# Polysketch attention and a noisy top-2 router on one core: batch 1's query features turned through DRAM, keys-values in one step, loads in another order, two buffers for the final reads

## The chip, the cores and the metric

One core of a Trainium2 chip runs the whole program. The metric is the device time of one execution in microseconds. All arrays begin and end in DRAM.

## The reference

Attention comes first. For each of 4 batches and 4 heads there are 1088 tokens with 32 numbers in q, k and v. Two 8 x 32 sketches S1 and S2 give 8 + 8 numbers for a token, and their outer product is its 64 features:

```python
def phi(x):
    a = np.einsum('rd,bhsd->bhsr', S1, x)
    b = np.einsum('rd,bhsd->bhsr', S2, x)
    return np.einsum('bhsi,bhsj->bhsij', a, b).reshape(*x.shape[:-1], r * r)
q_p, k_p = (phi(q), phi(k))
kv = np.einsum('bhsf,bhsd->bhfd', k_p, v)
z = np.sum(k_p, axis=2)
num = np.einsum('bhsf,bhfd->bhsd', q_p, kv)
den = np.einsum('bhsf,bhf->bhs', q_p, z)[..., None] + 1e-06
return (num / den).astype(np.float32)
```

The result is laid out as x with 4352 tokens of 128 numbers. The router then adds noise to x @ w_gate, scaled by log1p(exp(x @ w_noise)), takes the best two of 8 experts for each token and softmaxes their two numbers; each chosen expert adds its weight times relu(x @ w1[e]) @ w2[e], with w1 of 128 x 1024 and w2 of 1024 x 128.

## The kernel before

The program builds a list of jobs (`Plan.add`), and then issues them in one fixed order that is written out by hand: `PLACES` is that order as job numbers, `ENGINES` the engine of each job (P for PE, D DVE, A ACT, G POOL, S for SP, which issues DMAs), `ZEROS` the number of filler matmuls that PE runs ahead of a job (`idle`, L465 to L471), and `HOLDS` the loads that wait for a given scatter. Each engine runs its own jobs in that order, one after the other. SP's queue is in order too: a DMA that waits for data keeps back all that is behind it on SP.

A batch is 8 columns of 128 tokens (t = 0 to 7) and a half column (t = 8). For each batch:

- `load_kq` and `load_v` (L373 to L392) load k and q in one DMA each and v in six; all DMAs go through one helper (L351, issued at L356).
- `turned` (L617 to L625) puts tokens along the partitions with DVE's transpose.
- `sketches` (L627 to L682) multiplies by the sketches on PE (L640, L643), copies one half out (L349), makes the other (`ab`, L657), and forms the products (L675) on DVE or POOL: `phk` and `phq`, the features of k and q.
- `keys_values` (L708 to L790) runs these, copies v into `vaug`, and multiplies features by values on PE (L757), in five steps for batch 0 and three for the others; `fold` (L775) puts the gate weights into the result `kvw`.
- The numerators (L819) want the q features turned. By default PE turns them, two transposes for a column (L807), and an engine evicts them to `pT`. For the batches in `TURNED`, `squares` (L690 to L706) does it instead: four DMAs of 128 KB write four columns to DRAM, four read them back in rows of 128 bytes, and DVE transposes 32 x 32 blocks (L703).
- `queries` (L792 to L864) divides, and forms logits.
- `router` (L920 to L1102) takes the tokens of half a batch (a group w): counts of tokens for each expert by matmul (L1009, L1012), positions (L1030), the row of each token in the experts' buffer `xs` (L1049 to L1053), weighted copies `xg` (L1065, L1067), and indirect scatters on POOL into `xs` (L1093), each behind a `step` memset (L913).

The experts work on blocks of 128 rows of one expert (`block`, L1143 to L1259). The first four blocks (u = 0 to 3, issued in the order 0, 2, 1, 3) do not wait for scatters: one-hot squares (L1155, L1156, L1159) gather their rows from x on PE (L1165). Blocks below `QUICK` = 8 load their rows `xb` in one DMA with rows of 512 bytes, transpose on PE (L1184) and evict; later blocks load in four DMAs with rows of 128 bytes and transpose on DVE (L1194). Then PE multiplies by w1 (L1204, two steps of 8 matmuls), ACT or DVE applies relu (L1212, L1210), and PE multiplies by w2 (L1219, two steps). The results go by indirect scatter into `pairs` (L1247), and `sums` (L1263 to L1286) reads both rows of a token back as `pr`, adds them (L1277), adds what late blocks left in a PSUM bank (L1237, L1281), and writes the output. `blocks` is one tile that serves the one-hot squares, `squares` and `spread` in turn; `pr` has one buffer.

Of the kernel before, what the change touches and what calls it, by code (L numbers as in the profile page):

```python
# [101 lines left out]
TURNED = (2, 3)  # L102
HOLDS = {'clear6': (1, 2, 1), 'v3': (1, 2, 1)}
PLACES = [4, 3, 20, 33, 42, 43, 44, 21, 45, 1, 48, 50, 0, 56, 60, 24, 57, 49, 53, 51, 35, 52, 18, 63, 2, 61, 62, 36,
# [1417 lines left out]
```

## Time and profile before

| what | us |
|---|---|
| median of 3 runs (338.49 to 339.95) | 339.68 |
| the profiled execution | 339.91 |
| its span | 338.2 |
| PE busy in the span | 326.5 |
| POOL busy | 239.6 |
| DVE busy | 174.4 |
| ACT busy | 121.8 |

In the rows below a PE row is a group of matmuls that run one behind the other: start, duration, line, result<-operands, number, and in brackets the idle time ahead of it and what ended that. SPq rows are DMA issues. PEclk is the granted clock of PE as a share of full speed. The DMA share is the mean busy share of the core's 16 DMA engines.

### The profile page before, as it was taken

To read this page: it belongs to the slowest core of one execution; us is meant where nothing else is said; L and a number is where in the kernel's file an instruction comes from. 1 tells how busy PE (TensorE), PEld (TensorE's weight loads), DVE (VectorE), ACT (ScalarE), POOL (GpSimd) and SP (SyncE) were. 2 spreads that over 40 slices of the span, in tenths; PEclk is the share of its full clock that TensorE was granted. 3 is DMA by queue.
4 is the path that set the end of the run, shared out by engine and by line. 5 is a ranking of instruction groups with operands and counts; after the bars stand their busy time and mean duration, and the time that the engine had idled before them with its cause. 6 is when DMAs were issued, how large, how long until landed. Compare 5 with 4: busy or idle time off the path is not lost.

```text
span 338.2 us, 8094 instructions
## 1 busy us (share of the span) xinstructions
PE 326.5 (97%) x2848; PEld 311.4 (92%) x2848; DVE 174.4 (52%) x652; ACT 121.8 (36%) x325; POOL 239.6 (71%) x396
## 2 busy tenths in 40 slices
PE   8997999999999999999999999999999999999991
PEld 5885899999999999999999999999999999999991
DVE  5679975776748675473565544420223232423342
ACT  2366677345544443531333231123322212122310
POOL 7555487894876988498858888388878647766610
PEclk9799999999999999999999999999999999999998
DMA  7999994944563664465325166214534021323451
GB/s 169 270 281 297 240 293 127 297 121 92 108 163 67 129 143 91 67 162 96 71 55 84 43 141 142 78 35 114 87 65 96 33 90 52 106 80 112 136 178 52
DMA packets 91563, 42.81 MB, mean 127 GB/s; under 512 B 67141, under 2 KB 84934, under 8 KB 91520
## 3 DMA queue, kind: packets, MB, share of 16 engines
q1 hardware_dynamic: 86880, 33.25, 43.5%
q0 software_dynamic: 4544, 8.89, 7.4%
q8 instruction: 23, 0.38, 0.5%
q14 instruction: 20, 0.16, 0.2%
q10 hardware_dynamic: 96, 0.13, 0.1%
HBM read 26.27 MB, written 16.17 MB: 126 GB/s over the span
## 4 chain that ended last, share of the span: by engine, by line
PE 73%; DMA 8%; POOL 7%; issue 5%; DVE 4%; SPq 1%; ACT 1%; POOLq 0%; DVEq 0%
PE hp L1204 30%; PE acc L1219 29%; POOL pairs L1247 5%; PE bank L819 4%; PE bank L643 4%; POOL step L913 2%; DMA out_dram<-o 2%; DMA kq<-in_q_dram 2%; PE bank L757 2%; SPq L356 1%; DMA pr<-pairs 1%; PE turn L1165 1%; DMA xb<-xs 1%; PE bank L807 1%; DVE o L1277 1%
## 5 line engine op out<-in xcount | busy, mean ns | idle before, releaser
L1219 PE MATMUL acc<-w2s,h 128*128 128x128 f32 x1152 | 145.9, 275 | 0.0
L1204 PE MATMUL hp<-bT,w1s 128*128 128x128 f32 (+1 forms) x896 | 145.5, 306 | 0.1
L1219 PEld LDWEIGHTS acc<-w2s,h 128*128 128x128 f32 x1152 | 140.5, 192 | 2.6
L1204 PEld LDWEIGHTS hp<-bT,w1s 128*128 128x128 f32 x896 | 121.2, 192 | 5.0 <-ACT bT L349 0.4
L1212 ACT ACTIVATE h<-hp 128x512 f32<-128x512 f32 x104 | 62.0, 598 | 122.2 <-PE hp L1204 107.4
L1093 POOL DMA_INDIRECT xs<-xg,to x72 | 71.6, 994 | 34.8 <-issue 10.5
L1247 POOL DMA_INDIRECT pairs<-y,mine x70 | 69.7, 996 | 34.7 <-ACT y L349 18.2
L913 POOL MEMSET step<- 1x512 f32 x142 | 73.0, 514 | 0.1
L1210 DVE TENSOR_SCALAR h<-hp 128x512 f32<-128x512 f32 x40 | 27.7, 691 | 74.0 <-PE hp L1204 52.8
L349 ACT COPY y<-acc 128x128 f32<-128x128 f32 x52 | 13.2, 265 | 41.7 <-PE acc L1219 36.4
L1194 DVE STREAM_TRANSPOSE bT<-xb 128x128 f32<-128x128 f32 (+1 forms) x48 | 16.3, 347 | 7.0 <-PE hp L1204 3.8
L819 PE MATMUL bank<-kvw,pT 128*128 128x98 f32 x128 | 16.7, 272 | 0.0
L1065 ACT ACTIVATE xg<-x,g 128x128 f32<-128x128 f32 x49 | 16.0, 394 | 0.0
L819 PEld LDWEIGHTS bank<-kvw,pT 128*128 128x128 f32 x128 | 15.7, 192 | 0.0
L349 DVE COPY y<-acc 128x128 f32<-128x128 f32 x18 | 5.0, 282 | 18.7 <-PE acc L1219 18.1
L657 DVE TENSOR_TENSOR ab<-bank,lo 128x256 f32<-128x256 f32 (+2 forms) x17 | 6.3, 380 | 8.9 <-ACT lo L349 8.8
L1277 DVE TENSOR_TENSOR o<-pr 128x512 f32<-128x512 f32 (+1 forms) x12 | 6.5, 544 | 7.7 <-DMA out_dram<-o 6.1
L643 PE MATMUL bank<-sk,qTs 128*128 128x128 f32 x64 | 10.0, 296 | 0.0
L675 DVE TENSOR_TENSOR phq<-ab 128x512 f32<-128x512 f32 (+1 forms) x13 | 9.3, 717 | 0.1
L643 PEld LDWEIGHTS bank<-sk,qTs 128*128 128x128 f32 x64 | 8.9, 210 | 0.0
L471 PE MATMUL turn<-const-bfloat16-1.0 128*128 128x512 bf16 (+2 forms) x26 | 7.7, 447 | 0.9 <-PEq L1505 0.9
L349 ACT COPY pT<-bank 128x512 f32<-128x512 f32 (+1 forms) x12 | 6.2, 516 | 4.5 <-PE bank L807 4.4
(184 smaller groups left out, 277.5 us busy)
## 6 DMA issues: line engine op xcount, KB each, us to landing
w1s<-in_moe_w_dram SPq DMA_DIRECT2D x8, 512.0 KB
w2s<-in_moe_w_dram SPq DMA_DIRECT2D x8, 512.0 KB
pr<-pairs SPq DMA_DIRECT2D x8, 512.0 KB
kq<-in_k_dram SPq DMA_DIRECT2D x4, 544.0 KB
kq<-in_q_dram SPq DMA_DIRECT2D x4, 544.0 KB
vld<-in_v_dram SPq DMA_DIRECT2D x16, 128.0 KB
xb<-xs SPq DMA_DIRECT2D x128, 16.0 KB
there<-phq SPq DMA_DIRECT2D x16, 128.0 KB
```

The lines of the kernel that those rows point to most:

```text
L349: A.copy(o, i) if e == "ACT" else V.tensor_copy(o, i)
L643: T.matmul(ps.t[rows, 2 * W * i:2 * W * i + 2 * W], lhsT=lhsT, rhs=sk[:].rearrange("p c h x -> p (c h x)"), start=True, stop=True)
L819: T.matmul(ps2.t[:, c0:c0 + 2 * YW], lhsT=pT.t[:, at + P * (2 * i + a):at + P * (2 * i + a) + P], rhs=kvw.t[:, a, :], start=True, stop=True)
L913: job.fill = G.memset(step[:], 0.0)
L1065: A.activation(out=xg.t[:, i, c, 0:D], in_=x.t[:, c, :], func=AF.Copy, scale=B_["g"].t[:, i, c:c + 1])
L1093: ins = G.indirect_dma_start(out=xs[:], in_=xg.t[rows, i, t, :], in_offset=None, out_offset=bass.IndirectOffsetOnAxis(ap=to.t[rows, i, t:t ...
L1194: add("DVE", vec(P * n), lambda _: V.transpose(bT.t[:, 0:P * n], flat()), r=[xb], w=[bT], prio=TOP + u)
L1204: T.matmul(hp.t[:, P * n * i:P * n * (i + 1)], lhsT=w1s[:, e, P * (js * g + i):P * (js * g + i + 1)], rhs=bT.t[:, 0:P * n], start=True, st ...
L1210: V.tensor_scalar_max(h.t[:], hp.t[:], 0.0)
L1212: A.activation(out=h.t[:], in_=hp.t[:], func=AF.Relu)
L1219: T.matmul(acc.t[:, D * c:D * c + D], lhsT=h.t[:, P * (n * i + c):P * (n * i + c + 1)], rhs=w2s[:, e, j, :], start=(j == 0 and c == 0), st ...
L1247: ins = G.indirect_dma_start(out=pairs[:], in_=y.t[:], in_offset=None, out_offset=bass.IndirectOffsetOnAxis(ap=numbers_of[w].t[:, e, c:c + ...
```

## The change

- Batch 1 joins `TURNED`: its q features go through DRAM in two squares. `squares` and `spread` get a tile of their own (`squared`); `pr` gets a tile of its own and `blocks` as a second buffer.
- POOL products of batch 1 (`held`) wait until the index of group 0 is formed, and the index's last step (a CAST) of group 0 moves from DVE to POOL.
- Keys-values of batches 1 to 3 are one step instead of three.
- `QUICK` goes from 8 to 4: blocks 4 to 7 load in four DMAs and are transposed by DVE.
- In `sums` the adds of the PSUM banks at the end keep the order of the list (`summed`).
- `HOLDS`: v of batch 3 is no longer held, w2 of expert 7 is. `ZEROS`: 22 fillers instead of 26, at other places.
- `PLACES` and `ENGINES` are written anew. On SP, in the first 50 us: k0, q0, v0, k1, noise, w1 of expert 0, w1 of 2, a clear, w1 and w2 of 6, v1, q1, a clear, w2 of 0 and 1, k2, w2 of 3, w1 of 4 and 1, q2, the four stores of batch 1's first square with w1 of 3 among them, w2 of 2, w2 of 5, a clear. Before: k0, q0, v0, noise, w1 of 0, k1, q1, v1, w1 of 2, w2 of 1, w1 of 3, a clear, w1 of 1 and 7, w2 of 0, k2, w2 of 2, a clear, w2 of 4, a clear, the last piece of v1. (Small loads and the place of each piece of v are left out.) On PE the q features of columns 4 to 7 of batch 0 stand behind the fold instead of ahead of the keys-values. On POOL the product of columns 0 and 1 of batch 1's q features stands behind the first scatter of group 0 and two products of k features.

```diff
-TURNED = (2, 3)
-HOLDS = {'clear6': (1, 2, 1), 'v3': (1, 2, 1)}
+TURNED = (1, 2, 3)
+HOLDS = {'clear6': (4, 3, 1), 'w2_7': (0, 1, 0)}
...
-ZEROS = {44: 7.6, 50: 4.5, 153: 12, 222: 1}
+ZEROS = {44: 7.6, 66: 4.5, 72: 1.0, 153: 8}
...
-    tag("pr", 1, [P, 4, 2, D])
...
+    squared = const.tile([P, 1024], F32, name="squared")
+    kept("pr", const.tile([P, 4, 2, D], F32, name="pr"), blocks[:].rearrange("p (c k d) -> p c k d", c=4, k=2))
     kept("oh", *(blocks[:, 512 * i:512 * i + 512].rearrange("p (c x) -> p c x", c=4) for i in range(2)))
-    kept("squares", blocks[:].rearrange("p (i y x) -> p i y x", i=4, x=32))
-    kept("spread", blocks[:, 0:5 * P])
+    kept("squares", squared[:].rearrange("p (i y x) -> p i y x", i=4, x=32))
+    kept("spread", squared[:, 0:5 * P])
...
-            add(products, {"DVE": vec(256 * (m - i)), "POOL": gtt(256 * (m - i))}, product, r=list(source),
+            formed = add(products, {"DVE": vec(256 * (m - i)), "POOL": gtt(256 * (m - i))}, product, r=list(source),
                 w=[(jobs[i][2], jobs[x][1]) for x in range(i, m)], prio=prio, port={"DVE": 0.0 if whole == "PSUM" else 1, "POOL": 9})
+            if held and "POOL" in products:
+                behind_index.append(formed)
...
+            kw["held"] = b == 1
...
-        for ts in ((0, 1), (2, 3), (4, 5), (6, 7), (8,)) if head else ((0, 1, 2), (3, 4, 5), (6, 7, 8)):
+        for ts in ((0, 1), (2, 3), (4, 5), (6, 7), (8,)) if head else (tuple(range(C + 1)),):
...
-            V.tensor_copy(B_["to"].t[:, :, 0:n], B_["at"].t[:, :, 0:n])
+            if w > 0:
+                V.tensor_copy(B_["to"].t[:, :, 0:n], B_["at"].t[:, :, 0:n])
...
+        if w == 0:
+            pool_job(gps(2 * n) + 0.08, prio, lambda: G.tensor_copy(to.t[:, :, 0:n], B_["at"].t[:, :, 0:n]), [to], [B_["at"]])
+            indices.append(plan.jobs[-1])
...
-    QUICK = 8
+    QUICK = 4
+    summed = []
...
-                    in1=bank.t[rows, 0:c * D].rearrange("p (c d) -> p c d", d=D), op=ALU.add), r=[bank], w=[o], prio=prio)
+                    in1=bank.t[rows, 0:c * D].rearrange("p (c d) -> p c d", d=D), op=ALU.add), r=[bank], w=[o], prio=prio,
+                    after=summed)
+                summed.append(plan.jobs[-1])
...
+    for j in behind_index:
+        j.deps.update(indices)
     plan.write(idle)
```

## Rows read from the trace of the kernel before

**Rows 1.** The page, parts 1 and 4: busy time, chain that ended last.

```profile
PE 326.5 (97%) x2848; PEld 311.4 (92%) x2848; DVE 174.4 (52%) x652; ACT 121.8 (36%) x325; POOL 239.6 (71%) x396
...
PE 73%; DMA 8%; POOL 7%; issue 5%; DVE 4%; SPq 1%; ACT 1%; POOLq 0%; DVEq 0%
```

**Rows 2.** Windows: from:to, length, busy of each engine, PEclk, DMA share, GB/s.

```profile
2.00:50.00 48.00, 44.22 (x447) 38.14 (x446) 37.49 (x144) 26.32 (x84) 29.94 (x89) 0.96 1.00 268
...
50.00:330.00 280.00, 279.77 (x2392) 271.60 (x2389) 134.88 (x503) 94.90 (x242) 208.50 (x299) 1.00 0.45 106
...
12.00:16.00 4.00, 4.00 (x40) 3.88 (x42) 2.09 (x5) 2.23 (x7) 3.09 (x15) 0.67 1.00 340
16.00:20.00 4.00, 3.85 (x79) 3.26 (x75) 3.09 (x7) 2.16 (x6) 3.39 (x9) 1.00 0.76 233
36.00:40.00 4.00, 4.00 (x38) 4.00 (x38) 3.79 (x12) 1.49 (x7) 1.90 (x3) 1.00 0.88 191
104.00:112.00 8.00, 8.00 (x74) 8.00 (x73) 5.85 (x19) 3.37 (x10) 6.28 (x7) 1.00 0.61 101
```

**Rows 3.** Timeline of the end, PE and DVE.

```profile
330.13 1.38 PE L1237 MATMUL bank<-late_y,blocks 128*128 128x128 f32 x10 [0.35 <-ACT late_y L349]
331.01 0.69 DVE L1277 TENSOR_TENSOR o<-pr 128x512 f32<-128x512 f32 x1 [1.54 <-DMA pr<-pairs]
```

**Rows 4.** Timeline of PE, 10 to 60 us.

```profile
10.71 1.50 PE L640 MATMUL bank<-sk,qTs 128*128 128x64 f32 x8 [0.81 <-DVE qTs L623]
12.01 2.02 PE L643 MATMUL bank<-sk,qTs 128*128 128x128 f32 x8
...
21.25 1.04 PE L807 MATMUL bank<-ident,phq 128*128 128x128 f32 x8
22.12 1.95 PE L643 MATMUL bank<-sk,kTs 128*128 128x128 f32 x16
...
27.34 0.18 PE L1009 MATMUL bank<-mk,earlier 128*128 128x32 bf16 x1 [0.65 <-DVE mk L992]
...
40.99 0.86 PE L757 MATMUL bank<-phk,vaug 128*33 128x64 f32 x24 [0.65 <-issue]
...
44.78 1.06 PE L1219 MATMUL acc<-w2s,h 128*128 128x128 f32 x8
...
59.24 0.27 PE L1184 MATMUL turn<-ident,xb 128*128 128x128 f32 x1
```

**Rows 5.** Timeline of DVE: one-hot squares after the counts.

```profile
28.07 2.39 DVE L1159 TENSOR_SCALAR blocks<-place,pos,gm 128x128 f32<-128x128 f32 x3
...
38.14 0.34 DVE L1159 TENSOR_SCALAR blocks<-place,pos,gm 128x128 f32<-128x128 f32 x1
```

**Rows 6.** Timeline of SP and ACT: two issues, and the copy of v.

```profile
35.00 0.68 SPq L356 DMA_DIRECT2D vld<-in_v_dram  x1
...
39.83 1.06 ACT L349 COPY vaug<-vld 128x1024 f32<-128x1024 f32 x1 [1.24 <-DMA vld<-in_v_dram]
...
55.77 0.35 SPq L356 DMA_DIRECT2D xb<-xs  x1
```

**Rows 7.** DMA issues: what, queue, number, size of one.

```profile
w1s<-in_moe_w_dram SPq DMA_DIRECT2D x8, 512.0 KB
...
kq<-in_q_dram SPq DMA_DIRECT2D x4, 544.0 KB
...
there<-phq SPq DMA_DIRECT2D x16, 128.0 KB
...
xs<-pad SPq DMA_DIRECT2D x6, 258.0 KB
```

**Rows 8.** Timeline of POOL: group 0's first and last scatters, a product.

```profile
37.92 1.21 POOL L1093 DMA_INDIRECT xs<-xg,to  x1 [6.06 <-DVE blocks L1159]
...
40.81 1.08 POOL L675 TENSOR_TENSOR phq<-ab 128x512 f32<-128x512 f32 x1
...
51.08 0.96 POOL L1093 DMA_INDIRECT xs<-xg,to  x1 [0.17 <-issue]
```

More of the change, by code (lines that the diff above doesn't have):

```diff
@@ L194 @@
-ZEROS = {44: 7.6, 50: 4.5, 153: 12, 222: 1}
+TURNED = (1, 2, 3)
+HOLDS = {'clear6': (4, 3, 1), 'w2_7': (0, 1, 0)}
+PLACES = [20, 33, 21, 3, 4, 43, 44, 45, 29, 30, 25, 1, 26, 57, 49, 36, 48, 2, 39, 0, 56, 66, 67, 53, 54, 55, 22, 27,
[73 rows of a table added]
+ENGINES = (
+    "ASSSASSSGGGGGGSSSSSSGGGGGGGGGGGGGGGGGGGGGGDDPDAADDPADPADDDDDPADPADPADPADPADPPPPPAAPAADPDDGGPADGSSSSSSSSSSSSSSS"
+    "SSSSSSSSSSSSSSSSPAPDDADPAPDDAAAAAAGDDDDDDGAPDDGGDDGGAAAADDGGGGGGGGSDDDAADPADGGDDDPADDDPADDDDPDDGDSSSSSSSSDPAAP"
+    "AADPADDDSSSSSSSSDPAPDDPAPDDPAPDDAAAADDDDDDDDAPDDDGAADADDGGGGGGGGGGPDDPDDAAAADDDDDDDGAPDDDGADAADDGGGGGGGGPDDPDD"
+    "PAPDDAAAADDDDDDDDAPDDDGAAAADDGGGGGGGGGGSSSSSSSSAADPADDDDDDPADDDPADDDDPADDDSSSSSSSSDPDAPAADPADDDSSSSSSSSDPDDPDD"
+    "PDDPDDPAPDDAAAADDDDDDDDAPDDDGAAADAADDGGGGGGGGGGGGGGGGGGSSSSSSSSAADPADDDDDDPADDDPADDDDPDDDDSSSSSSSSDPDDPDADPADD"
+    "DSSSSSSSSDPDDPDDPDDPDDPDPDDAAAADDDDDDDDAPDDDGAAAAAADDGGGGGGGGGGGGGGGGGGGSDADDAPPPPAPAPPAPDGADDAPPPPAPAPPAPAGAA"
+    "AAPPPPAPAPPAPAGAAAAPPPPAPAPPAPAGSSSSDPAPPAPAGSSSSDPAPPAPAGSSSSDPAPPAPAGSSSSDPAPPAPAGSDDDSSSSDPAPPAPAGSSSSDPDPP"
+    "APAGSSSSDPAPPAPDGSSSSDPAPPAPDGSSSSDPAPPAPAGSSSSDPDPPAPDGSSSSDPAPPAPAGSSSSDPAPPAPAGSDDDDDDSSSSDPAPPAPAGSSSSDPDP"
+    "PAPDGSSSSDPAPPAPDGSSSSDPAPPAPAGSSSSDPAPPAPAGSSSSDPAPPAPDGSSSSDPAPPAPDGSSSSDPAPPAPDGSDSSDSSDSSDDDDDDSSSSDPAPPAP"
+    "AGSSSSDPAPPAPDGSSSSDPDPPAPAGSSSSDPAPPDPAGSSSSDPAPPAPAGSSSSDPAPPAPDGSSSSDPAPPAPAGSSSSDPAPPAPAGSSDDDDDDSSSSDPAPP"
+    "APPAPPAPAGAGSSSSDPDPPDPPAPPDPDGAGSSSSDPDPPDPPAPPDPAGDGSSSSDPAPPDPPAPPAPDGDGSSSSDPDPPAPPDPPDPAGAGSSSSDPDPPAPPAP"
+    "PAPAGAGSSSSDPAPPAPPDPPAPDGDGSSSSDPDPPDPPDPPDPDGDGSDSSDSSDSSSDDDDDDSSSSDPAPPAPPAPPAPDGDGSSSSDPDPPAPPAPPAPDGAGSS"
+    "SSDPAPPDPPDPPDPAGDGSSSSDPDPPDPPAPPDPDGAGSSSSDPAPPAPPDPPAPDGAGSSSSDPDPPAPPDPPAPDGDGSSSSDPAPPAPPAPPDPAGAGSSSSDPA"
+    "PPDPPAPPDPAGDGSDSSDSSDSSDSSSDDDDDDSSSSDPDPPDPAGSSSSDPAPPAPAGSSSSDPDPPAPAGSSSSDPAPPDPAGSSSSDPAPPAPAGSSSSDPAPPAP"
+    "AGSSSSDPAPPAPDAPPSSSSDPAPPAPDAPPSDDSSDDSA")
@@ L625, in turned, with sketches @@
         add("DVE", vec(128 * (c1 - c0) if c0 < C else 64), emit, r=[src], w=[(dst, c) for c in range(c0 // 2, -(-c1 // 2))], prio=prio)
-    def sketches(jobs, prio, whole=False, after=(), first=None, products=("DVE", "POOL"), bank="bank"):
+    def sketches(jobs, prio, whole=False, after=(), first=None, products=("DVE", "POOL"), bank="bank", held=False):
         ps = new(bank)
@@ L684 @@
     kv_of, kv_job = {}, {}
+    behind_index = []
     PQ = KNOBS
@@ L758, in emit @@
                                  start=(t == 0 and a == 0), stop=(t == C), skip_group_check=True)
-            kv_job[b] = add("PE", KV * len(ts), emit, lat=0.15, w=[kvp], prio=prio + 3.5,
+            kv_job[b] = add("PE", KV * len(ts) if head else 2.4, emit, lat=0.15, w=[kvp], prio=prio + 3.5,
                 r=[(pk, t) for t in ts] + [(va, 0), (va, 1)])
@@ L776, in fold @@
                              rhs=wg4[rows_of(l), a, :], start=True, stop=True)
-        folded = add("PE", 0.38, fold, lat=0.15, r=[kvT, "wg"], w=[ps], prio=prio + 3)
+        folded = add("PE", 0.58, fold, lat=0.15, r=[kvT, "wg"], w=[ps], prio=prio + 3)
         for l in range(2):
@@ L908 @@
     scatters = {}
+    indices = []
     def scatter_job(emit, **kw):
@@ L1052, in index @@
             V.tensor_reduce(out=B_["at"].t[:, :, 0:n], in_=B_["f2"].t[:, :, 0:n, :], axis=AX.X, op=ALU.add)
-            V.tensor_copy(B_["to"].t[:, :, 0:n], B_["at"].t[:, :, 0:n])
-        indexed = dve(0.2 + 2 * vec(16 * n), index, ["first", "row"], ["f2", "at", "to"], late)
+            if w > 0:
+                V.tensor_copy(B_["to"].t[:, :, 0:n], B_["at"].t[:, :, 0:n])
+        indexed = dve((0.2 if w > 0 else 0.0) + 2 * vec(16 * n), index, ["first", "row"], ["f2", "at"] + ["to"] * (w > 0), late)
         xg, to = B_["xg"], B_["to"]
+        if w == 0:
+            pool_job(gps(2 * n) + 0.08, prio, lambda: G.tensor_copy(to.t[:, :, 0:n], B_["at"].t[:, :, 0:n]), [to], [B_["at"]])
+            indices.append(plan.jobs[-1])
         pool_job(gps(18) + 0.1, prio, lambda: G.tensor_copy(xg.t[:, :, 0:n, D:XW].bitcast(I32), pid[:, :, b, t0:t0 + n].unsqueeze(3)),
```

16 lines of the change are left out of this document (removed), and 146 rows, old and new, of the table PLACES.

## The prediction

> **What bounds the kernel now.** I read the page first: PE is busy for 97% of the span, and the chain that ended last runs through PE for 73% and through DMA for 8% [rows 1]. The table of windows tells the two stages apart [rows 2]: from 50 to 330 us PE works 279.77 of 280 us, so there only PE work that disappears shortens the end; from 2 to 50 us it is idle for 3.8 us, and in that stage the 16 DMA engines are full (share 1.00 from 2 to 50 us, 268 GB/s). Whatever comes in this head as a wait or leaves it moves the whole later row of matmuls. The tail holds little: PE's last result needs 330.13 + 1.38 = 331.51, and DVE had the last read pairs in its hands at 331.01 [rows 3]. The profiled execution took 339.91 us, 338.2 of them the span; it stands 0.23 above the median of 339.68. I sum against 339.91 and subtract the same from 339.68.
>
> **PE work removed.** Eight transposes take 22.12 − 21.25 = 0.87 us, 0.109 each [rows 4]. Batch 1 loses 16 (columns 0 to 7 of its q features, two each), blocks 4 to 7 one each: 20 x 0.109 = **2.18 us**. Their evictions go too, off PE's path. In exchange DVE gets two transposes of a square and four of a block; DVE has 10.5 us of 48 free in the head [rows 2], so they cost nothing if the data is there; without that cover each is late by its own length. Keys-values in one step are the same matmuls: 0, between 0.65 gained (the wait ahead of the first third at 40.99 [rows 4]) and 0.65 lost if all of them now wait for the last product. Fewer fillers (26 to 22) cost or gain nothing by themselves: they stand in waits. The square's own tile lets it land while the one-hot squares are in use, v of batch 3 let loose and w2 of expert 7 held back move loads that PE needs 20 us and more later: 0.
>
> **The head.** Ahead of the counts of the first group of tiles (27.34) PE ran the q features of columns 4 to 7, 2.02 us at a low clock [rows 4], before the keys-values. They now stand behind the fold, in a stretch where PE waited or ran fillers. I take 2.0 us earlier counts, between 0 (if the values' copy holds the keys-values where they are) and 2.3. After the counts DVE formed three one-hot squares in 2.39 us beside three POOL products, where one alone took 0.34 [rows 5]: 2.39 − 3 x 0.34 = 1.37. The held products leave that stretch; I take 1.3, bounds 0 and 1.4. The index's CAST on POOL instead of DVE is 0.2 either way. The price of the hold is behind it, at the square's stores, below.
>
> PE order then reaches the w2 matmuls of the second block in order (block 2), the row at 44.78 [rows 4]. By the lists of the order, the changed kernel has done 1.2 us more PE work at that place (a w1 step of block 2 for one of block 1; two thirds of the keys-values 1.42 and two transposes of column 8, 0.22, that it has already done; less four transposes 0.44). So if X is the time at which it starts them, the end moves by X − 44.78 − 1.2 − 2.18 = **X − 48.16**, plus stalls that come later. By PE alone X = 44.78 − 2.0 − 1.3 − 0.65 + 1.2 = 42.0, a gain of 6.1.
>
> **But block 2 needs the w2 of its expert, and that is now late in SP's order.** Two things can hold it.
> First the bytes. The last v piece of batch 1 was issued at 35.00 and its copy could start at 39.83, 4.8 us later, having waited for it [rows 6]. Against what stood ahead of that piece, there stand ahead of and with block 2's w2 now four weight loads (w1 or w2 of an expert) of 512 KB more and two fewer, q of batch 2 (544), four stores of the square (128 each), and one clear less (258) [rows 7]: 1.87 MB more. At 340 GB/s, the rate from 12 to 16 us, this is 5.5 us, at the 268 of the whole head 7.0 [rows 2]: 45.3 to 46.8. Of idle DMA time 0.96 + 0.48 us can be filled (shares 0.76 and 0.88 [rows 2]): 43.9 to 45.4.
> Then the queue. SP issues in order, and the four stores of batch 1's first square, which wait for a POOL product of q features, stand in front of two weight loads. That product ended at 41.89 [rows 8], behind two scatters; now it stands behind one (some 1.65 less: 0.96, its step memset and 0.17 of issue), and what feeds it is 2.0 earlier: 38.2. Five issues of 0.43 and 4.8 to land: X = 45.2. Who waits: everything behind on SP (w1 of block 3, w2 of blocks 2 and 5), and PE. I take the later of both, X = 45.2: **−2.9**.
>
> **Later stalls.** The square's loads back have 128-byte rows. The window from 104 to 112, in which a square of batch 2 goes out and back with block loads beside it, has 0.61 x 8 = 4.9 us of all DMA engines [rows 2]; that is the upper bound for a square, the lower is 1.05 MB at 340 GB/s, 3.1. Loaded behind block 2's w2 and w2 of block 5, a clear and a piece of v, they are there about 7 us after X, with the DVE transpose; the numerators that need them come 11 us after X by PE's work: 0.
> Block 6 is next: its xb can only be read once the eight scatters of group 0 have landed. Before, the last ended at 52.04, the first read (of block 4, then first) was issued at 55.77 and transposed on PE at 59.24 [rows 4, 6, 8]. PE wants it at X + 13.5 = 58.7; it will be there between 59.5 and 3.3 us earlier. Stall 0 to 0.8: +0.4. Four issues of 0.43 where there was one lie in SP's free time.
>
> **Reads of the pairs in two buffers, ordered adds.** The second read can start before the first is added. PE's last result and the last read end within 0.5 us [rows 3], so 0, bounds ±0.3.
>
> **The clock.** PE idled 0.81 us before 10.71, and the granted clock of 12 to 16 us is 0.67 on average, so between the levels 1.2 and 2.4 GHz [rows 2, 4]: 4 x 0.33 = 1.3 us lost. It may happen again with fewer fillers or go away. From 16 to 20 us, with PE busy 3.85 of 4, it is back at 1.00 [rows 2]. I take 0, bounds ±1.3. The Trainium skill, "TensorE: Matmul & The Clock Gate", section What's actually happening, calls the throttled clock the default, which activity releases. The rows agree that it came back under work; by the rule every filler removed speaks against the change, and the sum would be −1.2 in place of −2.5; that fewer fillers lower the clock here, no run shows yet.
>
> **Sum:** −2.9 + 0.4 = −2.5: 337.4 against the profiled 339.91, **337.2** against the median. A measurement here tells 0.5% (1.7 us) from no change.
>
> **Rivals.**
> *Loads in time (0.20).* The DMA is full at 268 GB/s but moved 340 for 4 us, so the bytes ahead may pass faster, and SP may reach the stores only after the product is done. Then X = 42.0, block 6 is wanted at 55.5 and ready at 56.2 at best: −6.1 + 0.7 = −5.4, about 334.3. Against it: a share of 1.00 over the whole head.
> *Nothing reaches the end (0.22).* X = 45.4 by the lower rate, block 6 no earlier than before (59.5 instead of 58.9: +0.6) and one more drop of the clock (+1.3): −2.8 + 0.6 + 1.3 = −0.9, about 338.8. This is the change that doesn't do what it says: the transposes' 2.18 us are freed and waited away. Some 0.08 of the chance is the clock's, since the one drop before followed an idle PE.
> *Slower (0.18): SP stands at the square's stores.* POOL's first scatter waits for tiles weighed on ACT, which forms one-hot squares at that time, and the product, now behind two held products and that scatter, holds the stores, the weights behind them, and so PE. Each us that the product is late is one of PE's. It decides at a product's end of 48.16 − 7.0 = 41.2; before, it ended at 41.89 [rows 8] with counts 2 us later. If it ends at 43.0, X = 50.0: +1.8, about 341.5; the gap that then opens on PE (8 us from its own 42.0) may lower the clock and add up to 1.3. For it speaks that POOL's first scatter waited 6 us before; against it that most of what it waited for moves forward with the counts.
>
> **How the numbers follow.** Forecast 0.40 (X from 44 to 46.4, 335.5 to 338.0), the rivals 0.20, 0.22 and 0.18. All of the forecast and the first rival is faster by over 0.5%: 0.60; the second is within it, 0.22; the third 0.18. The range reaches down past the first rival's middle by 0.5 and up to just short of the slower one's: 333.8 to 341.0; it leaves out some 0.1 on either side. The forecast's own range is 335.5 to 338.0.
>
> **What would show it.** Step by step: 20 fewer transposes in the PE rows of L807 and L1184; counts at about 25.3; three one-hot squares on DVE in about 1 us; block 2's second matmuls (L1219) released by DMA of w2s, not by ACT, at about 45; the POOL product ahead of the stores ending at about 38; block 6's first matmuls at about 59 after a wait of under 1 us on a DMA or DVE transpose; from there to 329 us no idle PE. The prediction is wrong if block 2's second matmuls start before 43 or after 48, if PE waits for the numerators of batch 1, or if a stall of over 1 us appears after 65 us.

## The result, and the profile after

| | before | after |
|---|---|---|
| median (lowest to highest), us | 339.75 of 6 (338.49 to 342.61) | 335.58 of 6 (334.23 to 337.13) |
| the profiled execution | 339.91 | 335.77 |
| its span | 338.2 | 334.1 |
| end of PE's last matmul in it | 331.51 | 328.83 |
| from there to the span's end | 6.69 | 5.27 |

The ratio is 0.9878, with an interval of 0.9842 to 0.9913: faster, by more than the 0.5% that counts as a difference here. (A ratio, here and below, leaves out executions over 1.5% above the fastest of the same kernel.) Sign and range held, but the gain is 4.2 us where 2.5 were forecast. The last two lines of the table say where to look: 2.68 us come from PE's row, which the sum was about, and 1.42 from the time behind it, which the sum had put at nothing.

The lines have moved: w1 is L1214 now, w2 L1229, the keys-values L762, the numerators L824, the counts L1015, the gathers L1175, the products of features L676, the sums' adds L1289 and L1293. The page of after, parts 1 and 4, against [rows 1]:

```profile
PE 323.3 (97%) x2822; PEld 308.7 (92%) x2824; DVE 175.4 (53%) x653; ACT 125.4 (38%) x334; POOL 238.4 (71%) x398
...
PE 81%; DVE 6%; SPq 4%; DMA 4%; issue 2%; ACT 1%; POOL 0%; DVEq 0%
```

PE has 3.2 us less to do. Its part of the chain that ended last grew from 73% to 81%, while POOL's fell from 7% to 0 and DMA's from 8% to 4%. Windows of after (columns as in [rows 2]):

```profile
2.00:50.00 48.00, 44.52 (x453) 39.19 (x453) 38.98 (x151) 28.28 (x89) 32.43 (x95) 0.96 1.01 275
50.00:326.00 276.00, 275.20 (x2352) 266.94 (x2351) 134.56 (x499) 96.34 (x245) 204.78 (x294) 1.00 0.49 114
20.00:30.00 10.00, 7.37 (x45) 5.83 (x45) 9.05 (x43) 7.27 (x28) 5.37 (x14) 0.84 1.11 290
```

The head is as full of DMA as before, and PE is idle in it for 3.5 us (3.8 before). New is the third row: from 20 to 30 us PE is idle for 2.6 us, and the granted clock is 0.84 on average, so part of the time it stood at 1.2 instead of 2.4 GHz. The drop of before, at 12 us, is gone: from 10 to 20 us the clock is 1.00 in after and 0.83 in before. The timeline of PE in after shows the places, to be read against [rows 4]:

```profile
24.82 0.19 PE L1015 MATMUL bank<-mk,earlier 128*128 128x32 bf16 x1 [0.66 <-DVE mk L998]
...
26.93 0.80 PE L1175 MATMUL turn<-blocks,x 128*128 128x128 f32 x2 [1.82 <-ACT blocks L1166]
27.52 1.87 PE L824 MATMUL bank<-kvw,pT 128*128 128x98 f32 x8
...
42.48 2.21 PE L762 MATMUL bank<-phk,vaug 128*33 128x64 f32 x72
44.84 1.13 PE L1229 MATMUL acc<-w2s,h 128*128 128x128 f32 x8 [0.16 <-DMA w2s<-in_moe_w_dram]
...
58.65 1.98 PE L1214 MATMUL hp<-bT,w1s 128*128 128x128 f32 x16
...
63.88 2.02 PE L1214 MATMUL hp<-bT,w1s 128*128 128x128 f32 x16 [0.58 <-PE acc L1229]
```

Counts at 24.82 (25.3 was forecast), block 2's second matmuls at X = 44.84, released by the DMA of their weights (45.2), block 6 at 58.65 with no wait (59): the steps of the head stand where the sum put them. Not foreseen are the 1.82 us ahead of the gathers, where PE waits for a one-hot square of ACT; the eight numerators behind them take 1.87 us instead of 1.03, so the clock has fallen there. The wait that was expected at block 6 stands at block 4 instead, 0.58 us at 63.88.

Why the weights came when they came is on SP; the timeline of SP in after:

```profile
36.00 0.81 SPq L355 DMA_DIRECT2D there<-phq  x2
36.86 0.42 SPq L355 DMA_DIRECT2D w1s<-in_moe_w_dram  x1
37.33 0.91 SPq L355 DMA_DIRECT2D there<-phq  x2
38.28 1.43 SPq L355 DMA_DIRECT2D w2s<-in_moe_w_dram  x2
```

SP stood at the stores until 36.00, as the forecast had it, and went on to the w2 of block 2 at 38.28. What let it go is seen on DVE and POOL (timeline of after):

```profile
27.79 0.34 DVE L1169 TENSOR_SCALAR blocks<-place,pos,gm 128x128 f32<-128x128 f32 x1
28.15 2.08 POOL L676 TENSOR_TENSOR phk<-ab 128x512 f32<-128x512 f32 x2
28.21 1.02 DVE L1090 TENSOR_TENSOR lim<-stops,reach 128x8 f32<-128x8 f32 x1
...
33.90 2.04 DVE L676 TENSOR_TENSOR phq<-ab 128x512 f32<-128x512 f32 x1
34.30 1.08 POOL L676 TENSOR_TENSOR phq<-ab 128x512 f32<-128x512 f32 x1
```

POOL's product, which the forecast had ending at 38.2, ended at 35.38; the last one ahead of the stores was DVE's, 2.04 us long and done at 35.94. The chain that ended last goes through it (the chain of after):

```profile
33.98 1.96 DVE phq L676
46.34 4.71 DMA xs<-xg,to
55.03 4.55 DMA xb<-xs
74.67 2.23 DMA xb<-xs
```

It does not go on through the stores, w2 and X. From the product it runs through DVE's next steps to the last scatter of group 0, then through SP's reads of rows for the blocks, and comes to PE only at 77.56, at a last wait of 0.22 us. So in after the end hangs on these reads: behind the 0.16 at X they take 0.58 and 0.22 us from what PE has gained.

The two one-hot squares that DVE still makes here take 0.34 us each, as forecast for three; the held POOL products have moved on to other instructions of DVE (L1090, 1.02 us for 128 x 8 numbers). PE does not wait for these, but the product ahead of the stores does: it stands behind them on DVE, which names no wait between the counts and that product.

Last the end. Timeline of before, the rows beyond [rows 3]:

```profile
331.81 0.69 DVE L1281 TENSOR_TENSOR o<-o,bank 128x512 f32<-128x512 f32 x1
332.42 0.27 DVE L1277 TENSOR_TENSOR o<-pr 64x128 f32<-64x128 f32 x1
...
332.73 0.28 DVE L1281 TENSOR_TENSOR o<-o,bank 64x128 f32<-64x128 f32 x1
```

and of after:

```profile
327.04 0.89 DVE L1289 TENSOR_TENSOR o<-pr 64x128 f32<-64x128 f32 x2 [1.14 <-DMA pr<-pairs]
...
327.45 1.38 PE L1247 MATMUL bank<-late_y,squared 128*128 128x128 f32 x10 [0.35 <-ACT late_y L348]
327.98 0.28 DVE L1293 TENSOR_TENSOR o<-o,bank 64x128 f32<-64x128 f32 x1
...
328.87 0.69 DVE L1293 TENSOR_TENSOR o<-o,bank 128x512 f32<-128x512 f32 x1 [0.61 <-PE bank L1247]
329.59 0.66 ACTq L355 DMA_DIRECT2D out_dram<-o  x1
```

Before, the adds of the small piece stood behind those of the large one, and its output was issued last, at 333.74 (the end of SP's last issues), 2.23 us after PE's end. After, the small piece is done while PE still works, and the last issue is the large one, ended at 330.25, 1.42 after PE's end. That is 0.81 of the 1.42 us. Of it, 0.26 is the bank's add of the large piece, which follows PE's end by 0.30 before (331.81; DVE was still adding the read) and by 0.04 after (328.87). The other 0.61 is the landing of the last output: 4.46 us from that issue to the span's end before, 3.85 after.

### The profile page after: what moved, and what is told of

Read it like the earlier page. It is cut to its first block, busy times and chain, and to the rows that moved or that the text cites. A ratio compares the mean times of both kernels' runs of the same rounds, so it can differ in the third digit from the quotient of the medians.

```text
span 334.1 us, 8083 instructions
## 1 busy us (share of the span) xinstructions
PE 323.3 (97%) x2822; PEld 308.7 (92%) x2824; DVE 175.4 (53%) x653; ACT 125.4 (38%) x334; POOL 238.4 (71%) x398
## 4 chain that ended last, share of the span: by engine, by line
PE 81%; DVE 6%; SPq 4%; DMA 4%; issue 2%; ACT 1%; POOL 0%; DVEq 0%
PE acc L1229 34%; PE hp L1214 34%; SPq L355 4%; PE bank L824 3%; DMA xb<-xs 2%; PE bank L644 2%; PE turn L472 2%; DMA xs<-xg,to 1%; PE bank L762 1%; PE bank L641 1%; PE hp L641 1%; PE bank L1247 1%; DVE phq L676 1%; PE acc L762 1%; DVE phk L676 1%
## 5 line engine op out<-in xcount | busy, mean ns | idle before, releaser
L1229 PE MATMUL acc<-w2s,h 128*128 128x128 f32 x1152 | 145.4, 276 | 0.2 <-DMA w2s<-in_moe_w_dram 0.2
L1214 PE MATMUL hp<-bT,w1s 128*128 128x128 f32 (+1 forms) x896 | 144.8, 306 | 0.8 <-PE acc L1229 0.6
L1229 PEld LDWEIGHTS acc<-w2s,h 128*128 128x128 f32 x1152 | 140.1, 192 | 2.8 <-issue 0.3
L1214 PEld LDWEIGHTS hp<-bT,w1s 128*128 128x128 f32 x896 | 121.1, 192 | 5.8 <-PE acc L1229 1.1
L1257 POOL DMA_INDIRECT pairs<-y,mine x70 | 68.7, 982 | 33.5 <-issue 11.0
L1220 DVE TENSOR_SCALAR h<-hp 128x512 f32<-128x512 f32 x38 | 26.3, 691 | 65.7 <-PE hp L1214 53.5
L1204 DVE STREAM_TRANSPOSE bT<-xb 128x128 f32<-128x128 f32 (+1 forms) x52 | 17.6, 343 | 15.1 <-DMA xb<-xs 11.9
L348 ACT COPY y<-acc 128x128 f32<-128x128 f32 x42 | 10.7, 263 | 37.0 <-PE acc L1229 33.4
L1075 ACT ACTIVATE xg<-x,g 128x128 f32<-128x128 f32 x65 | 21.0, 392 | 0.3 <-DMA pairs<-y,mine 0.3
L348 DVE COPY y<-acc 128x128 f32<-128x128 f32 x28 | 7.6, 282 | 20.8 <-PE acc L1229 15.4
L824 PE MATMUL bank<-kvw,pT 128*128 128x98 f32 x128 | 17.3, 282 | 0.0
L824 PEld LDWEIGHTS bank<-kvw,pT 128*128 128x128 f32 x128 | 16.4, 201 | 0.0
L676 DVE TENSOR_TENSOR phq<-ab 128x512 f32<-128x512 f32 (+1 forms) x14 | 10.0, 723 | 0.1
L644 PE MATMUL bank<-sk,qTs 128*128 128x128 f32 x64 | 9.2, 279 | 0.6 <-DVE den L839 0.6
L644 PEld LDWEIGHTS bank<-sk,qTs 128*128 128x128 f32 x64 | 8.0, 192 | 0.9 <-PE bank L824 0.8
L707 DVE STREAM_TRANSPOSE pT<-squared 128x1024 f32<-128x1024 f32 x6 | 7.4, 1241 | 1.5 <-DMA squared<-there 0.8
L676 DVE TENSOR_TENSOR phk<-ab 128x512 f32<-128x512 f32 (+1 forms) x13 | 8.0, 614 | 0.0
```

What stands on the lines that cost most here:

```text
L348: A.copy(o, i) if e == "ACT" else V.tensor_copy(o, i)
L644: T.matmul(ps.t[rows, 2 * W * i:2 * W * i + 2 * W], lhsT=lhsT, rhs=sk[:].rearrange("p c h x -> p (c h x)"), start=True, stop=True)
L676: (G if e == "POOL" else V).tensor_tensor(out=jobs[i][2].t[rows, jobs[i][1]:jobs[m - 1][1] + 1, :, :].rearrange("p c h (i j) -> p (c h) i ...
L824: T.matmul(ps2.t[:, c0:c0 + 2 * YW], lhsT=pT.t[:, at + P * (2 * i + a):at + P * (2 * i + a) + P], rhs=kvw.t[:, a, :], start=True, stop=True)
L1075: A.activation(out=xg.t[:, i, c, 0:D], in_=x.t[:, c, :], func=AF.Copy, scale=B_["g"].t[:, i, c:c + 1])
L1214: T.matmul(hp.t[:, P * n * i:P * n * (i + 1)], lhsT=w1s[:, e, P * (js * g + i):P * (js * g + i + 1)], rhs=bT.t[:, 0:P * n], start=True, st ...
```

## The experiments

They ran on three chips, one for each group below, with the kernel before on the same chip; all edits are made to the kernel after. The kernel after as it stands ran beside them on the third chip only; where the first two groups compare with it, they compare with the result above. In the pieces of the order, a number is a job.

### First chip: what sets X, and what X is worth

**w2_ahead** issues the w1 of block 3 and the w2 of block 2 (jobs 104 and 103) ahead of the square's stores:

```diff
-633, 206, 205, 208, 210, 661, 104, 209, 196, 207, 103, 162,
+633, 206, 205, 104, 103, 208, 210, 661, 209, 196, 207, 162,
```

> The changed kernel with w1 of block 3 and w2 of block 2 issued on SP ahead of the four stores of batch 1's first square, nothing else moved. In the changed kernel SP stood at these stores until 36.00, when DVE's product ended, and PE waited 0.16 us for w2 of block 2 at 44.84. Theory (SP's stand sets that landing): the wait of PE on w2s is gone, w2 lands 2 us or more earlier, block 2's w2 matmuls start at 44.7, and the end moves by only -0.2, because PE itself came at 44.68. Rival (the bytes in front set it): the start stays at 44.8 and PE still waits on the DMA. Second rival (something else is freed): over 1 us faster.

It gave 334.05, ratio 0.9858 (0.9785 to 0.993), span 333.0. Timeline of PE:

```profile
44.99 1.16 PE L1229 MATMUL acc<-w2s,h 128*128 128x128 f32 x8
```

The wait for the weights is gone, and X has not moved forward (44.99 against 44.84): PE gets there by its own work no earlier. But the clock was low for longer in this execution (0.81 from 20 to 30 us, 0.85 from 30 to 40, against 0.84 and 0.99 in after), so PE itself came later. In after weights and PE arrive within 0.2 us of each other (the wait of 0.16).

PE's end came 1.09 us earlier all the same (327.74 against 328.83), since the later waits of after, 0.58 and 0.22 us, are not in this trace. There the chain that ended last runs on PE through the whole stretch from 60 to 83 us, and no longer through the reads. That is the second rival of the expectation (something else is freed) and not its theory. One trace of each shows it; the ratios, 0.9858 and 0.9878, don't tell the two kernels apart.

**fill** puts seven filler matmuls into the wait ahead of the gathers:

```diff
-ZEROS = {44: 7.6, 66: 4.5, 72: 1.0, 153: 8}
+ZEROS = {44: 7.6, 66: 4.5, 72: 1.0, 153: 8, 628: 7}
```

> The changed kernel with 7 more filler matmuls ahead of the first gather, in the 1.82 us in which PE idled at 25.1 to 26.9 and after which its numerators ran at about half speed (1.87 us for 8 instead of 1.03). Theory (PE and the load of w2 are tied at 44.8): the clock stays up, PE comes to block 2's w2 about 1.0 us earlier and waits there about 1.2 us; the end stays (within 0.3). Rival (the clock's fall is on the path): about 1.0 us faster.

It gave 333.3, ratio 0.9821 (0.9779 to 0.9863), span 332.1. Timeline of PE:

```profile
26.52 0.49 PE L1175 MATMUL turn<-blocks,x 128*128 128x128 f32 x2 [0.28 <-ACT blocks L1166]
26.85 1.03 PE L824 MATMUL bank<-kvw,pT 128*128 128x98 f32 x8
...
43.36 1.13 PE L1229 MATMUL acc<-w2s,h 128*128 128x128 f32 x8 [0.16 <-DMA w2s<-in_moe_w_dram]
```

The granted clock from 20 to 30 us is 1.00, the numerators take 1.03, and X moved forward by 1.48, weights included. The theory that PE would only wait longer for its weights fell: the stores go at 34.53 instead of 36.00, w2 is issued 1.41 earlier, and lands 1.48 earlier. Two things make up these 1.47 us. The counts, which stand ahead of the fillers, came 0.40 earlier in this execution (24.42 against 24.82), so that part is not the fillers'. The rest is the length of DVE's product, the last one ahead of the stores (timelines of POOL and DVE):

```profile
32.85 1.06 POOL L676 TENSOR_TENSOR phq<-ab 128x512 f32<-128x512 f32 x1 [0.42 <-DVE den L839]
33.45 1.02 DVE L676 TENSOR_TENSOR phq<-ab 128x512 f32<-128x512 f32 x1
```

In after POOL's product ran inside DVE's time and DVE's took 2.04; here it began first and DVE's took 1.02. POOL was earlier because its scatter waits for ACT (0.30 us here, 1.74 in after), and ACT for PE's transposes (its copy starts at 28.38, in after at 30.32). So the stores follow PE by way of ACT, POOL and DVE, and are not a fixed date. The span fell by 2.0 us, some 1.6 without the counts' part.

The ratios of fill and after (0.9821 and 0.9878) were not measured side by side, and their intervals overlap. The granted clock of whole executions says the same as the traces: 0.996 to 0.998 in the four of fill, 0.985 to 0.994 in the six of after; and the one execution of w2_ahead with 0.996 took 332.96.

**w2_fill** has both edits.

> Both edits: the two weight loads ahead of the stores and the 7 fillers. Theory (two limits tied): only both together pay: block 2's w2 matmuls start at about 43.7 and the end comes 1.1 us earlier than that of the changed kernel, about 334.5. Rival (bytes): start 44.8, wait on w2s of about 1 us, no gain. Rival (clock alone): as much as the fillers alone.

It gave 333.32, ratio 0.9828 (0.9785 to 0.9872), span 331.3, X at 43.13 with no wait: no more than fill by itself can be told. With fill it is the fastest version seen on this chip; by the ratios to the kernel before it is some 0.5% better than the result of the change.

**late_store** does what the slower rival described: POOL's product ahead of the stores goes behind two more scatters, and the stores and the weights behind them follow it.

```diff
-633, 206, 205, 208, 210, 661, 104, 209, 196, 207, 103, 162,
+633, 206, 661, 196, 162,
...
+641, 168, 205, 208, 210, 104, 209, 207, 103, 116, 211, 643,
```

> The changed kernel with POOL's product of batch 1's q features (columns 0 and 1) behind two more scatters, and the stores of the square with all that follows them on SP after it. The slower rival of the prediction in small: the product ends at about 38.7 instead of 35.4 (the stores then come at 38.75 instead of 36.00). Theory (each us that the stores are late is one of PE's): block 2's w2 matmuls start at about 47.6, the end is 2.7 us later. Rival (loads already in flight hide it): start under 46, end under 1 us later.

It gave 336.79, ratio 0.994 (0.9909 to 0.997), span 335.0. Timelines of PE and SP:

```profile
37.04 0.81 SPq L355 DMA_DIRECT2D there<-phq  x2
...
45.47 0.79 PE L1229 MATMUL acc<-w2s,h 128*128 128x128 f32 x5 [2.34 <-ACT g L1010]
```

The stores came at 37.04, not at the 38.75 expected, and X at 45.47, not 47.6. The wait of 2.34 is put down to ACT's `g`, which can't be it: in after these matmuls start 1.1 us ahead of that instruction (45.95). The weights are left, issued from 39.32.

Against after the stores are 1.04 later, X 0.63 and the span 0.9, which by size is the expectation's rival. But the clock stayed at 1.00 from 20 to 40 us here without the fillers, so fill is the fairer measure: stores 2.51 later (37.04 against 34.53), X 2.11 later, PE's end 2.91 later (329.77 against 326.86), 3.5 us more by medians. Not all of this is the weights'. Behind the wait the clock fell (window of late_store):

```profile
40.00:50.00 10.00, 7.66 (x111) 7.29 (x111) 5.23 (x33) 3.58 (x11) 5.43 (x9) 0.83 1.00 261
```

Laid side by side with fill, matmul by matmul, PE is 2.11 later at X, 3.6 later at 49.6 us, and 2.9 at the end, where fill has small waits that late_store has not. So a us at the stores costs 0.84 us at X, and the clock can come on top, as the prediction's slower rival had it; the change doesn't meet that rival, because its product is early enough.

### Second chip: single parts of the change undone

These four carry the seven fillers of fill. None of them gains here: each ratio to the kernel before is near 1, where fill had 0.982 on the first chip; the whole change was not run on this chip. They are read against one another and by the rows of their part.

**tail_order** undoes the order of the last adds:

```diff
-                    after=summed)
...
-1576, 1572, 1573, 1577,
+1576, 1572, 1577,
...
-1570, 1574, 1575, 1571, 1578, 1580, 1579,
+1570, 1571, 1578, 1580, 1579, 1573, 1574, 1575,
```

> The changed kernel with the 7 fillers ahead of the first gather (for a steady clock; its span without further edits was 332.1) and the last adds in the order of the kernel before: the large read and its bank first, the small piece behind it. Theory (the order of the last adds gave the 1.4 us that the tail gained beyond PE): the last add ends 1.2 to 1.5 us after PE instead of 0.7, and the span is 0.8 to 1.4 longer, 333.1. Rival (the tail gained because the reads land earlier against PE's end): span within 0.3 of 332.1.

It gave 340.74, ratio 1.0 (0.9972 to 1.0029), span 339.9. Timeline of the end:

```profile
334.28 0.69 DVE L1293 TENSOR_TENSOR o<-o,bank 128x512 f32<-128x512 f32 x1 [0.88 <-PE bank L1247]
334.89 0.28 DVE L1289 TENSOR_TENSOR o<-pr 64x128 f32<-64x128 f32 x1
335.00 1.20 SPq L355 DMA_DIRECT2D out_dram<-o  x2
335.00 0.66 ACTq L355 DMA_DIRECT2D out_dram<-o  x1
335.20 0.28 DVE L1293 TENSOR_TENSOR o<-o,bank 64x128 f32<-64x128 f32 x1
```

The old picture is back: the small piece last, and the last issue ended at 336.20, 1.96 us after PE's end at 334.24 (1.42 in after and fill, 2.23 in before). So the order is worth 0.54 us, less than the theory's 0.8 to 1.4. The other 0.27 of the 0.81 remains with the order undone: the large read is there and added before PE's end, as in after. The span ends 5.66 after PE, 5.24 in fill, but that holds the landing of the last output too.

**one_pr** gives `pr` one buffer:

```diff
-    kept("pr", const.tile([P, 4, 2, D], F32, name="pr"), blocks[:].rearrange("p (c k d) -> p c k d", c=4, k=2))
+    kept("pr", const.tile([P, 4, 2, D], F32, name="pr"))
```

The reads are issued as in after, each ahead of the adds of the one before it, so some sums add rows of the later read. The run leaves out the wait that one buffer brings with it in before, a read that stands back until the adds are done.

> The same base with one buffer for the reads of the pairs instead of two. Theory (the second buffer gives nothing): the last large read is issued at about the same time, since the add before it ends some 2 us ahead of that issue; span 332.1 to 332.4. Rival (the two buffers gave the tail's gain): the read lands after PE's last result and the span is 1 us or more longer.

It gave 341.49, ratio 1.0014 (0.998 to 1.0047), span 340.2. The last issue ends 1.42 after PE's end, as with two buffers, and the span 5.62 after it. This prices nothing, since the wait was left out; what the second buffer is worth was not shown. If it is what lets the last large read land early, it is worth the 0.27 above at most.

**not_held** lets the two held POOL products of batch 1 go ahead of the index:

```diff
-        j.deps.update(indices)
+        pass
...
-154, 192, 153, 155,
+154, 192, 153, 186, 187, 155,
...
-631, 186, 240, 241, 222, 187, 110,
+631, 240, 241, 222, 110,
```

> The same base with the two held POOL products of k features back ahead of the index, and nothing made to wait. Prediction's term: the one-hot squares on DVE take up to 1.1 us each beside them, the first gather and all behind it come 1.0 to 1.3 us later, span 333.2. Rival (the hold moves the cost: two small DVE steps after the index took 1.0 us each in the changed kernel beside these products, and would be fast again): within 0.4 of 332.1.

It gave 340.96, ratio 1.0019 (0.9984 to 1.0055), span 338.1. Timeline of PE:

```profile
25.97 0.19 PE L1015 MATMUL bank<-mk,earlier 128*128 128x32 bf16 x1 [2.15 <-DVE mk L998]
```

and of POOL:

```profile
23.78 2.08 POOL L676 TENSOR_TENSOR phk<-ab 128x512 f32<-128x512 f32 x2
```

The counts come at 25.97, against 24.49 to 24.77 in the other three. That is not the forecast's 1.3, though near it in size: in before the products stood behind the counts, from 28.30, beside the one-hot squares; here they start ahead of the counts and are over when the squares come, which took 0.34 here too. What they slow is DVE's work ahead of the counts (`mk` took 0.95 instead of 0.19). So the run shows that the products must not stand ahead of the counts, and doesn't test the term of the squares. On DVE the price is the same early or late: its product ahead of the stores starts at 33.51 here, and at 33.45 in fill. The medians don't tell whether it reaches the end, since what follows differs by more among these four.

**no_square** takes batch 1 out of `TURNED` again, so that PE transposes its 8 columns, ahead of their numerators, and ACT evicts them (the order, with new job numbers, is left out here):

```diff
-TURNED = (1, 2, 3)
+TURNED = (2, 3)
```

> The same base with batch 1 out of the turned batches: 16 transposes on PE and their evictions on ACT in place of two squares (16 DMAs, 2 transposes on DVE); the rest of the order stands, the transposes stand ahead of their numerators, and the turn of column 8 behind them. Theory (transposes are PE time and nothing else pays for the squares): 16 x 0.109 = 1.75 us more after 50 us, while w2 of block 2, no longer behind the stores, gives 0.2 back: span 333.7. Rival (the squares cost in the head what they save: SP stood 2 us at their stores and the DMA engines were full): block 2 starts 1 us or more earlier, span within 0.6 of 332.1.

It gave 341.5, ratio 1.0029 (1.0002 to 1.0057), span 342.2. X is 45.50, 1.4 and 1.0 earlier than in tail_order and one_pr, and PE's end 335.61, 1.4 and 1.0 later. From X on PE needs 2.0 to 2.8 us more, where the 16 transposes by themselves are 1.75. So with the squares X is 1.0 to 1.4 later on this chip, which takes back half of what they save. But nearly all of that is halts of PE within the keys-values, which the third chip takes up: the row begins at 40.88 here, and at 41.06 and 41.35 with the squares. What the squares cost where PE doesn't halt was not shown.

### Third chip: why the gain is not there on every chip

Much of the time lost on the second chip is on PE, in the middle of the row that the change had merged: in tail_order PE is 3.6 us behind fill at the end of that row, and 7.4 at its own end. So on a third chip the kernel after ran as it is, beside versions that split the keys-values again.

**again** is the kernel after with no edit.

> The changed kernel itself, unedited, on the chip of this call. The kernels with one-step keys-values gave two pictures: 72 matmuls in 2.21 us without a gap on one chip, and on another, after some 51 of them, groups of two or three with 0.4 to 0.6 us between them, in which PE waited for nothing but issue, and the whole gain gone. If the second picture belongs to the chip and not to the four edits, this kernel shows the one that this chip gives: span 333 to 334 without gaps, 338 or more with them.

It gave 343.69, ratio 0.9978 (0.9938 to 1.0018), span 342.5: no gain that can be told. (The kernel before spread from 339.49 to 349.40 on this chip, so the ratios here are less firm than on the first.) Timeline of PE:

```profile
43.12 1.87 PE L762 MATMUL bank<-phk,vaug 128*33 128x64 f32 x60
45.45 0.28 PE L762 MATMUL bank<-phk,vaug 128*33 128x64 f32 x2 [0.47 <-issue]
...
47.16 0.28 PE L762 MATMUL bank<-phk,vaug 128*33 128x64 f32 x2 [0.66 <-issue]
...
48.90 1.16 PE L1229 MATMUL acc<-w2s,h 128*128 128x128 f32 x8
```

The same 72 matmuls, one step of 2.21 us in after, take 5.8 us: after 60 of them PE halts five times for half a us, and the profile names nothing that it waits for ("issue"). X is 4.06 later, 0.64 of it ahead of this row, where the clock was low for longer (0.83 from 30 to 40 us, 0.99 in after). The waits of again say how often:

```profile
PE bank L762 <- issue: 3.6, 8, 0.7
```

Eight halts, five here and three in batch 2's keys-values at 92 us; there the delay against after grows from 3.6 to 5.4. The rest is lost before the last numerators, as the views of L824 show. In after:

```profile
L824 PE MATMUL bank<-kvw,pT x128: 250/275/422, 27.5 to 170.5; 128*128 128x98 f32 x128
```

and in again:

```profile
L824 PE MATMUL bank<-kvw,pT x128: 250/275/421, 27.5 to 179.0; 128*128 128x98 f32 x128
```

Both start the first numerators at 27.5; the last start at 170.5 and 179.0, and from there PE's end is 158.3 us away in both (328.83 and 337.27). The 8.4 us lie in the attention's stage alone, about 5 of them in these two steps. Laid side by side, matmul by matmul, most of the rest comes in rows of w1 and w2 behind the later keys-values: 0.6 us at 100.5, 1.4 from 150.9 to 154.7, 0.7 from 171.5 to 174.5.

**kv_spread** makes the keys-values of batches 1 to 3 three steps again, with large matmuls between them:

```diff
-        for ts in ((0, 1), (2, 3), (4, 5), (6, 7), (8,)) if head else (tuple(range(C + 1)),):
+        for ts in ((0, 1), (2, 3), (4, 5), (6, 7), (8,)) if head else ((0, 1, 2), (3, 4, 5), (6, 7, 8)):
```

> The changed kernel with keys-values of batches 1 to 3 in three steps again, each 24 matmuls with eight or more large matmuls between them (for batch 1: a third, a sketch of batch 2, a third, block 2's w2, a third). Theory (a long row of small matmuls outruns the supply of instructions to PE where the DMA engines are full): where the unedited kernel has gaps, these go and the span falls by 3 us or more; where it has none, the two agree within 0.5 us. Rival (the gaps come from something else in that stretch): the gaps stay, in the thirds or in the matmuls after them.

It gave 340.11, ratio 0.9919 (0.9878 to 0.9959), span 338.1, 4.4 less than again; part of this is the clock, which was low for less time here (0.88 and 0.95 from 20 to 30 and 30 to 40 us, 0.83 and 0.83 in again). Its waits (lines one higher):

```profile
PE acc L1230 <- issue: 1.5, 4, 0.5
...
PE bank L763 <- issue: 0.8, 2, 0.4
```

With the 1.0 us that again has at L1229 as well, half of the halted time is gone, and most of what is left stands in the w2 matmuls between the thirds.

**w2_fill_2** is w2_fill once more, on this chip.

> The version with two weight loads ahead of the stores and 7 fillers, again on this chip. Without gaps: 331.3 as before. With gaps in the one-step keys-values: 336 or more, and about 2 us under the unedited kernel.

It gave 342.62, ratio 1.0036 (0.9997 to 1.0075), span 340.7. PE reaches the keys-values 2.1 us earlier than in again (41.03), halts there as long, and the clock falls in the halts (0.83 from 40 to 50 us). What gave 2 us on the first chip gives nothing that can be told here.

**all_three** is w2_fill with the keys-values in thirds.

> That version with keys-values in three steps as well. Theory: 331 to 332 on any chip, the fastest of the four where there are gaps. Rival (three steps cost something by themselves): 0.5 us or more above the version without them where there are no gaps.

It gave 340.22, ratio 0.9962 (0.9932 to 0.9992), span 339.3. The expectation of one and the same time on any chip missed by 8 us; the halts are still there (1.2 us at w2, 1.1 in the keys-values). Splitting gains the same in both pairs, by the means of the executions that the ratios compare: 342.9 to 340.7 from again to kv_spread, 342.8 to 340.4 from w2_fill_2 to all_three. So the one step costs some 2.2 us on this chip, and something else beside it holds PE's issue here that splitting doesn't reach.

What that is stays open. One of the 23 packets of 16 KB on the queue that the page calls "instruction" falls into or right behind the first keys-values with halts (45.42 us, for 1.14) and without (44.83, for 1.11), so these packets alone don't tell the chips apart. The kernel before wasn't profiled on the second and third chip, so where it loses time there isn't known; its medians, 339.13, 340.65 and 344.46 on the three chips, say that it loses some as well.

## Why the prediction was right, and where it wasn't

**The relation X − 48.16** held within 0.2 us. With X = 44.84 it gives −3.32; two small waits that came later (0.58 at 63.88 and 0.22 at 77.56) leave −2.52, and PE's end moved by −2.68. But X did not decide alone: with the wait at 77.56 still to come, an X that is a little earlier by itself would have been waited away there. The terms under it stand too: 26 fewer matmul records, 20 transposes and 4 fillers among them; counts 0.5 earlier than forecast; keys-values 2.21 us.

**X itself** was right by luck: two errors cancel. The stores were let go at 36.00, not 38.2, and by a product of DVE, which the sum did not look at: POOL's first scatter waited 1.74 us instead of 6.06 [rows 8] and its product was done by 35.38, DVE's by 35.94. And w2 took 6.56 us from its issue to PE (38.28 to 44.84), not 4.8; the 4.8 came from a piece of v of 128 KB at 35.00 [rows 6], where this is 512 KB behind the stores. In fill it is 6.49 (36.87 to 43.36), and in late_store 6.15 (39.32 to 45.47), so 6.2 to 6.6 is the figure for this place.

**"By PE alone X = 42.0"** was wrong. With its weights there in time PE came at 44.99 (w2_ahead), or at 43.13 with the clock up (w2_fill): 1.86 goes with the clock, 0.19 of it already at the counts. From the counts to X, w2_fill needs 18.7 us (24.42 to 43.13), where the sum had 16.7 (25.3 to 42.0). The 1.3 us that the held products were to give back are missing from it: the second gathers follow the counts by 3.3 us in w2_fill and by 3.2 in before, since PE waits for a one-hot square of ACT now, a wait that fillers fill but don't shorten. Waits of 0.24 and 0.61 for DVE's `den` come behind it. So the rival *loads in time* failed at PE, not at the loads: weights in time alone moved X by nothing. A time below its 334.3 was reached by fill, through the clock.

**The clock, "0, bounds ±1.3"**, held against before, but by exchange: the drop at 12 us is gone (0.83 from 10 to 20 us in before, 1.00 in after) and a new one came at 27 (1.00 from 20 to 30 us in before, 0.84 in after). What the sum did not see is that the new one need not be: numerators took 1.87 behind an idle PE and 1.03 behind fillers, and the span fell by some 1.6 us. The Trainium skill, "TensorE: Matmul & The Clock Gate", section What's actually happening, has activity release the throttle; that work in the gap keeps the clock up agrees with fill (0.84 to 1.00). But late_store had the same gap of 1.82, no fillers, and the clock at 1.00 from 20 to 40 us: the drop is not certain in each execution.

**Block 6, +0.4**, became +0.58 at block 4, and not because of the scatters. Block 6 had its rows in time. "Four issues of 0.43 where there was one lie in SP's free time" is what failed: w1 loads and stores stand between block 4's four reads, the last of which is issued at 57.0, and the DVE transpose that PE needs came at 63.47.

**The tail, "0, bounds ±0.3"**, is the term that was mis-sized: it gave 1.42. The sum looked at the second buffer and at when the read lands, and not at the edit beside it, the order of the last adds. That order is 0.54 by tail_order; 0.27 is the last large read, added before PE's end now (whether by the second buffer was not shown), which is within the bounds; 0.61 is the landing of the last output, which took 3.7 to 5.2 us in these runs and belongs to no edit that was shown. So the size of the gain, 4.2 where 2.5 were forecast, owes the last 0.61 to luck.

**Slower, with SP at the stores:** the mechanism is real, 0.84 us at X for one us at the stores and the clock behind it (late_store), and its condition was not met: products were done at 35.94, and it decides at 41.2.

**"Keys-values in one step: 0"** holds where the result was measured and on the first chip, and fails on two others, where PE halts in the step of 72 for 0.2 to 0.7 us at a time; thirds took 2.2 us off on the one chip where they were tried. The bound of 0.65 was for a wait on a product; that PE's own issue could run dry had no place in the sum, and no row of before showed it there beyond the 0.65 of [rows 4], which already said "issue".

## What to carry to other kernels

Where a store waits in an in-order queue ahead of loads, ask what feeds the store: here it was a product on DVE, whose length hung on POOL's work beside it and so, by way of ACT, on the engine that waited for the loads; work moved forward on PE moved the loads as well. A short idle stretch of PE in a full head costs its length and can cost the clock behind it, which seven fillers gave back here (some 1.6 us on the first chip; on the third, together with the weights ahead, nothing that could be told). Of several waits the last one sets the end: with the weights ahead of the stores X did not move, and the end came 1.1 us earlier, since two later waits were gone. A long step of very small matmuls can halt PE on one chip and not on another; spread it among large ones, and don't take a gain of 1% for settled before a second chip has shown it.

## What was not expected of the hardware

The same kernel gained 1.2% on one chip and nothing that can be told on another, with every engine's program the same: halts of PE of 0.33 to 0.66 us, once some 60 small matmuls had gone by, and then after every two or three, while the DMA engines were full (share 1.07 from 40 to 50 us in again, 1.09 in after, which has no halts).

DVE's small additions on 128 x 8 numbers took 1.02 and 0.99 us beside POOL's products, and 0.13 and 0.17 where those had gone ahead (not_held). The Trainium skill, "SBUF — State Buffer", section SBUF: two separate sides, lets the vector engine's operations with two SBUF inputs and GpSimd's reads of SBUF shut each other out for a whole instruction; one product takes 1.04, and the trace agrees. DVE's product of 128 x 512 numbers is the dearer case: 2.04 us in after, with POOL's product inside its time, 1.02 in fill, where POOL's began first, and 0.68 in late_store, where POOL's came behind it; and it stands ahead of the stores.
